# Batch 0 of an FFT-then-GLU kernel: the input in three slices, one sum in column tiles, weight merges placed earlier

## The chip, the cores and the metric

One core of a Trainium2 chip runs the whole program. The metric is device time in microseconds (us). The kernel before took 1947.11 us, the median of three runs (1946.08 to 1948.29). One execution was also taken by the hardware profiler; every duration below is from that execution. The engines are PE (TensorE, matrix products; PEld is its weight loading), DVE (VectorE), ACT (ScalarE), POOL (GpSimd) and SP (SyncE, which here only issues DMAs).

## The reference

For `x` of 8 batches x 3008 positions x 256 features it takes the real part of a two-dimensional Fourier transform (over positions and over features), and sends every resulting row through a gated layer with 1536 hidden features:

```python
X = np.fft.fft(x, axis=1)
X = np.fft.fft(X, axis=2)
x = X.real.astype(np.float32).reshape(B * S, D)
gate = 1.0 / (1.0 + np.exp(-(x @ w_gate)))
out = (gate * (x @ w_val)) @ w_out
```

The three weight matrices come as 8-byte floats.

## The kernel before

**Mathematics.** The transform over features is a 256 x 256 product, so it is multiplied into `w_gate` and `w_val` once: `merge` (L329) makes the tables `G1` and `G2`. The transform over positions is done for each batch: the rows of x are folded (s, S-s, M+s and M-s added and subtracted, M = 1504), and the folded rows are multiplied with a cosine and a sine table `st`, which gives `pk` and `qk`. One feature column (number 128) of the cosine part has no partner; its transform, the row E, is kept apart. For a chunk of 252 frequencies and a tile of 128 hidden features, gate and value are then the sum of three terms: G1 times pk, plus E times a column `ge`, plus or minus G2 times qk. The two signs are the frequency and its mirror image.

**The loop.** The main loop (L917) goes over *steps* i. A step is one tile of 128 of the 1536 hidden features (12 a chunk) for one chunk of one batch. Steps 0 to 11 are the first chunk of batch 0. In a step, PE runs `front_a(i)` (G1 times pk, into a PSUM bank `pf`), `back` (five of the products with `w_out`, into the banks `po`; from step 5 on) and `front_b(i)` (G2 times qk). ACT takes twice the bank between the two (`part`, L616), and after front_b the sigmoid of one sign (`gate_a`, L635); DVE makes the other sign out of both (`z`, L640), multiplies gate and value (`h`, L652), ACT makes the second sigmoid (L653), DVE multiplies again (L654, called *second h* below). When the second h of step i is done, the bank of step i is free. POOL adds blocks of h (`sf`, L660) for a scheme that saves products: seven sums after steps 1, 4, 7..., six after steps 2, 5, 8....

**PSUM.** There are eight banks: three in the pool tagged `x`, used by `pf`, by merges and by the sums of the transform, and five named `po0` to `po4`, which `back` takes from step 5 on. Before that, other work may be put into them (the argument `other`).

**Weights.** There are 18 loads of 512 KB, each a tile of 256 columns of `w_gate` or `w_val`, or 256 rows of `w_out`, in the order of the list `jobs`. A load is made into 4-byte floats by `weight_parts` (two ACT instructions, L297 and L298) and `weight_join` (three DVE instructions, L307, L308 and L310, then one on POOL, L312). `weight_use` then merges it (four products, a copy of each half to SBUF on ACT, L336 and L337, and two small DMAs `ge` that turn row 0 of G2 into columns), or, for `w_out`, queues `forms`, sums of it for the saving scheme.

**Batch 0 in the kernel before.** x comes in two DMAs, the table in two halves each for cosine and sine (`load_table`, L192). DVE and POOL fold it in two halves (`half1`, `half2`). Six sums of the transform follow: for each of two blocks pk, E and qk. E is computed as if its one column were 128 equal ones, so its row stands on all partitions. In steps 0 to 4 E is added by two further products of G2 with a tile that has only row 0 filled; in steps 5 to 11 DVE adds it (`part`, L619, two instructions); from step 12 on ACT writes E times ge into the bank ahead of front_a (`seed`, L600).

**What sets the order.** All engines run their instructions in the order in which the program issues them; nothing reorders them at run time. The order of `pre`, `use` and `side` (L863 to L871) says in which step a join, a merge or a load stands. Loads are issued on SP, also in order; a DMA also waits until the one that used the same one of eight completion counters has landed, so a `ge` that is slow to land holds a load that has its counter.

Of the kernel before, what the change touches and what calls it, by code (L numbers as in the profile page):

```python
# [82 lines left out]
def kernel(  # L83
# [61 lines left out]
    def load_x(b):  # L145
        X[b] = xp.tile([P, 4, NQ, D], F32, name="x4", tag="x4")
        for h in range(0, 4, 2):
            if b:
                nc.sync.dma_start(out=X[b][:, h : h + 2], in_=XR[b][:, h : h + 2])
            else:  # L150
                nc.sync.dma_start(out=X[b][0:NP, h : h + 2], in_=xf[b, :, h : h + 2])
# [29 lines left out]
    G1 = const.tile([P, 2, F], F32, name="G1")  # L181
    G2 = const.tile([P, 2, F], F32, name="G2")
# [9 lines left out]
    def load_table(t, nq):  # L192
        for q in range(0, NQ, nq):
            yield nc.sync.dma_start(out=ST[0][0:NP, t, q : q + nq], in_=stab[:, t, q : q + nq])
# [14 lines left out]
    def table_odd():  # L209
# [21 lines left out]
        def tangent():  # L231
# [8 lines left out]
    jobs = [(0, 0), (1, 0), (0, 1), (1, 1), (2, 0), (0, 2), (1, 2), (2, 1), (0, 3), (1, 3), (0, 4), (2, 2),  # L240
            (1, 4), (0, 5), (1, 5), (2, 3), (2, 4), (2, 5)]
    RAW, WS = {}, {}
    shared = {}
    KEEP = 10

    def weight_load(j):


        w, c = jobs[j]
        src = (moe_w_gate, moe_w_val, moe_w_out)[w]  # L250
        src = src[2 * c * P : 2 * (c + 1) * P, :] if w == 2 else src[:, c * WC : (c + 1) * WC]
        src = src.rearrange("(c p) f -> p c f", p=P)

        def some(n, pool, tag):

            if tag not in shared:
                shared[tag] = pool.tile([P, n * WC], F32, name=f"w{tag}", tag=tag)
            return shared[tag]

        def home(j):  # L260

            if j in (0, 1, 2, 3, 5):
                if j > 2:
                    ws = some(5, pqp, "qk")[:, (j // 5) * 2 * WC : (j // 5 + 1) * 2 * WC]
                    return sp.tile([P, 4 * WC], F32, name="raw", tag="sf"), ws
                t = hp.tile([P, 6 * WC], F32, name="raw", tag="h")
                return t[:, 0 : 4 * WC], t[:, 4 * WC :]
            if j in (4, 6, 9):
                t = wf[:, {4: 1, 6: 2, 9: 3}[j]].rearrange("p m n -> p (m n)")
                return t[:, 0 : 4 * WC], t[:, 4 * WC : 6 * WC]  # L270
            t = some(10, cp, "c")
            if j == 7:
                raw = pqp.tile([P, 4 * WC], F32, name="raw", tag="pk")
                return raw, t[:, 6 * WC : 8 * WC]
            return t[:, 0 : 4 * WC], t[:, 4 * WC : 6 * WC]

        if j < KEEP:
            raw, ws = home(j)
        else:
            both = some(24, xp, "x4").rearrange("p (i n) -> p i n", n=2 * WC)  # L280
            r, i = (j - KEEP) % 3 * 2, 6 + (j - KEEP) % 6
            raw, ws = both[:, r : r + 2].rearrange("p a n -> p (a n)"), both[:, i]
        raw = raw.bitcast(I32).rearrange("p (c f w) -> p c f w", c=2, w=2)
        ws = ws.rearrange("p (c f) -> p c f", c=2)
        WS[j] = ws
        if src.dtype == F32:
            nc.sync.dma_start(out=ws, in_=src)
        else:
            RAW[j] = raw
            nc.sync.dma_start(out=raw.rearrange("p c f w -> p c (f w)"), in_=src.bitcast(I32))  # L290
# [38 lines left out]
    def merge(ws, g, c, other):  # L329
# [6 lines left out]
        nc.scalar.copy(G2[:, g, cs], ps[:, WC : 2 * WC])  # L336
        nc.scalar.copy(G1[:, g, cs], ps[:, 0:WC])  # L337
# [48 lines left out]
    def fold_ops(b, nq):  # L386
# [51 lines left out]
        else:  # L438

            def half1(q):  # L440
                point(nc.vector, 2, 3, q)
                first(nc.vector, 2, 3, q)
                for blk in range(2):
                    across(nc.vector, blk, q)
                    feat(nc.vector, *parts[blk], q)

            def half2(q):
                across(nc.vector, 0, q)
                feat(nc.vector, *parts[0], q)
                across(pool, 1, q)  # L450
                feat(pool, *parts[1], q)
            for q in qs:
                point(nc.vector, 0, 1, q)
            first(nc.vector, 0, 1, slice(0, NQ))
            point(pool, 2, 3, qs[1])
            first(pool, 2, 3, qs[1])
            ops += [lambda: half1(qs[0]), lambda: half2(qs[1])]
        for blk, (v, r) in enumerate(parts):
            if b and blk:
                W[b, blk] = v[:, :, HD:D], r[:, :, HD:D]  # L460
                continue
            W[b, blk] = (v[:, :, 0:HD], r[:, :, 0:HD],
                         v[:, :, HD : HD + 1].to_broadcast([v.shape[0], NQ, P]))
# [56 lines left out]
    def seq_start(b):  # L520
        PQE[b] = [pqp.tile([P, NK + 1], F32, name=name, tag=name) for name in ("pk", "qk")]
        if not b:
            PQE[b].append(op.tile([P, NK + 1], F32, name="ek", tag="os"))
# [5 lines left out]


# [60 lines left out]
    N1 = 5  # L591

    def seed(i):
# [5 lines left out]
        for g in range(2 if i >= NFT else 0):  # L599
            nc.scalar.activation(PF[i][:, g], EK[i // NFT], AF.Copy, scale=ge[:, g, f : f + 1])  # L600

    def front_a(i):
        (pk, *_), ks, _, _, fs = cut(i)
        if i < NFT:
            seed(i)
        for g in range(2):
            mm(PF[i][:, g], G1[:, g, fs], pk[:, ks], i < NFT and g == 0, True)
        for g in range(2 if i < N1 else 0):
            mm(PF[i][:, g], G2[:, g, fs], shared["qk"][:, 4 * WC : 4 * WC + CH], False, True)

    def part(i):
# [3 lines left out]
        if not N1 <= i < NFT:  # L615
            nc.scalar.activation(AP[i], PF[i], AF.Copy, scale=2.0)  # L616
            return
        for g in range(2):
            nc.vector.scalar_tensor_tensor(out=AP[i][:, g], in0=pqe[2][:, ks],  # L619
                                           scalar=ge[:, g, f : f + 1], in1=PF[i][:, g],  # L620
                                           op0=ALU.mult, op1=ALU.add)
# [6 lines left out]
    def gate_a(i):  # L628
# [7 lines left out]
        if N1 <= i < NFT:  # L636
            nc.vector.scalar_tensor_tensor(out=z[:, :, ::-1], in0=AP.pop(i), scalar=2.0, in1=PF[i],
                                           op0=ALU.mult, op1=ALU.subtract)
        else:
            nc.vector.tensor_tensor(z[:, :, ::-1], AP.pop(i), PF[i], op=ALU.subtract)  # L640
# [6 lines left out]
    def gate_b(i):  # L647
# [5 lines left out]
        nc.scalar.activation(pf[:, 0], z[:, 0], AF.Sigmoid)  # L653
        nc.vector.tensor_tensor(h[:, fh, n:], pf[:, 0], z[:, 1], op=ALU.mult)  # L654
# [145 lines left out]

    nc.gpsimd.memset(nil, 0.0)
# [3 lines left out]
    for j in range(2):  # L805
        weight_load(j)
    load_x(0)
    for _ in load_table(0, NQ // 2):
        pass
    for j in range(2, 5):  # L810
        weight_load(j)
    sines = load_table(1, NQ // 2)
    next(sines)
    for j in range(5, 7):
        weight_load(j)
    next(sines)
    for j in range(7, KEEP):
        weight_load(j)

    def weight_round(*js):  # L820
        for j in js:
            weight_parts(j)
            weight_join(j)

    weight_parts(0)
    weight_parts(1)
    weight_join(0)
    weight_join(1)
    weight_use(0)
    weight_use(1)  # L830
    seq_start(0)

    e0 = shared["qk"][:, 4 * WC : 4 * WC + CH]
    nc.gpsimd.memset(e0, 0.0)
    other = {(0, 0): (4, None), (0, 1): (4, None), (0, 2): (0, 1), (1, 2): (2, 3)}
    cos = [seq_group(0, blk, what, other.get((blk, what))) for blk in range(2) for what in (0, 2)]
    for i, f in enumerate(fold_ops(0, NQ // 2)):
        f()
        for sums, _, _ in cos:
            sums(*range(i * NQ // 2, (i + 1) * NQ // 2))  # L840
    sin = [seq_group(0, blk, 1, other.get((blk, 1))) for blk in range(2)]
    for i in range(2):
        for sums, _, _ in sin:
            sums(*range(i * NQ // 2, (i + 1) * NQ // 2))
    evacuate = [then for _, then, _ in cos + sin]
    for then, js in zip(evacuate, ((2, 3), (4,), (5,), (6,), (7,), (8,))):
        weight_round(*js)
        then()()
    nc.scalar.dma_start(out=ed[0:1], in_=PQE[0][2][0:1])
    nc.vector.tensor_copy(e0[0:1], PQE[0][2][0:1, 0:CH])  # L850
    weight_parts(9)
    for j in range(KEEP, KEEP + 3):
        weight_load(j)
    weight_use(2)
# [8 lines left out]
    pre, use = {}, {}  # L863
    for j, i in enumerate((0, 1, 2, 3, 4, 5, 6, 7, 9), 9):
        if i:
            pre.setdefault(i - 1, []).append(lambda j=j: weight_parts(j))
        pre.setdefault(i, []).insert(0, lambda j=j: weight_join(j))
        if KEEP <= j < len(jobs) - 3:
            at(i, lambda j=j: weight_load(j + 3))
    for j, i in enumerate((0, 0, 1, 2, 0, 3, 4, 5, 4, 6, 7, 8, 8, 8, 11), 3):  # L870
        use.setdefault(i, []).append(lambda j=j: weight_use(j))  # L871
    at(N1 - 1, lambda: nc.vector.tensor_copy(PQE[0][1][0:1, 0:CH], PQE[0][2][0:1, 0:CH]))
# [17 lines left out]
    for i in range(i0, count, i0):  # L890
        at(i - 8, lambda i=i: e_rows(i))
# [25 lines left out]
    for i in range(count):  # L917
        front_a(i)
        if N1 <= i < NFT:
            part(i)  # L920
        if i:
            gate_a(i - 1)
        if not N1 <= i < NFT:
            part(i)
        if i0 <= i + 1 < count:
            seed(i + 1)
        if i:
            gate_b(i - 1)
# [67 lines left out]
```

## Time and profile before

| | |
|---|---|
| Median of three runs | 1947.11 us |
| The profiled execution's own time | 1951.1 us |
| Its span | 1949.0 us |
| PE busy | 1917.7 us (98% of the span) |
| POOL, DVE, ACT busy | 82%, 75%, 68% |
| PE busy in the first 1/40 of the span (48.7 us) | 6 tenths |
| Start of the first front_a, step 0 | 52.57 us |
| Start of front_b of step 14 | 120.88 us |
| One step where PE never waits | 3.125 us |

The page divides the span into 40 slices. PE is busy for nine tenths or more in all but the first. From 121 us on, the chain that ended last is PE alone for a long way: eight matmul records of `pf` (1.70 us) and ten of `po` (1.43 us) in turn, 3.125 us a step. A product of 4-byte floats is recorded as two matmuls, so "x8" is four products.

### The profile page before, as it was taken

How to read it: one execution, taken by the hardware profiler on the slowest of the kernel's cores; microseconds unless marked ns; L12 is line 12 of the kernel's file. 1: busy time of each engine (PE TensorE's matmuls, PEld its weight loads, DVE VectorE, ACT ScalarE, POOL GpSimd, SP SyncE). 2: the span in 40 equal slices, each digit the busy share in tenths (PEclk: the TensorE clock that was granted, in tenths of full speed). 3: DMA queues.
4: the chain of work that ended last, by engine and by line, in shares of the span. 5: the costliest groups of instructions: out<-in, count | busy, mean ns of one | idle time of the engine just before them, and what ended most of it. 6: DMA issues, size and time to landing. Idle time of an engine off the chain costs nothing.

```text
span 1949.0 us, 34556 instructions
## 1 busy us (share of the span) xinstructions
PE 1917.7 (98%) x11262; PEld 1789.8 (92%) x11262; DVE 1461.0 (75%) x3269; ACT 1332.5 (68%) x3125; POOL 1589.7 (82%) x2842
## 2 busy tenths in 40 slices
PE   6999999999999999999999999999999999999999
PEld 3789889999999999999999999999999999999998
DVE  6777787787777777777777777777777777776776
ACT  3567757776777677776777767777677776777775
POOL 3779998997889878987889878888788886777775
PEclk8999999999999999999999999999999999999999
DMA  8352513212012120222012021221210110011101
GB/s 270 90 145 20 118 32 111 47 25 82 14 47 58 17 79 14 57 49 79 14 25 78 18 79 23 45 53 20 82 20 14 19 23 14 14 20 22 25 16 31
DMA packets 168565, 97.85 MB, mean 50 GB/s; under 512 B 131803, under 2 KB 160070, under 8 KB 165838
## 3 DMA queue, kind: packets, MB, share of 16 engines
q1 hardware_dynamic: 167254, 95.12, 20.5%
q8 instruction: 91, 1.49, 0.3%
q14 instruction: 88, 0.72, 0.1%
q10 hardware_dynamic: 1100, 0.51, 0.1%
q0 software_dynamic: 32, 0.00, 0.0%
HBM read 70.35 MB, written 47.24 MB: 60 GB/s over the span
## 4 chain that ended last, share of the span: by engine, by line
PE 92%; DVE 4%; DMA 2%; ACT 1%; issue 0%; SPq 0%; ACTq 0%; DVEq 0%
PE pf L135 48%; PE po L135 40%; PE ev L135 3%; DMA st<-in_stab_dram 1%; DVE c L754 1%; PE od L135 1%; DMA ge<-G 1%; PE ps L135 1%; DVE z L640 1%; ACT pf L653 0%; DVE h L654 0%; DVE h L652 0%; PE row L135 0%; DVE wf L375 0%; DMA raw<-in_moe_w_val_dram 0%
## 5 line engine op out<-in xcount | busy, mean ns | idle before, releaser
L660 POOL TENSOR_TENSOR sf<-h 128x168 f32<-128x168 f32 (+1 forms) x955 | 530.8, 574 | 225.1 <-DVE h L654 225.0
L660 POOL TENSOR_TENSOR sf<-h,sf 128x168 f32<-128x168 f32 (+1 forms) x1146 | 638.4, 576 | 61.5 <-DVE h L654 60.9
L135 PE MATMUL pf<-qk,G 128*128 128x252 f32 (+1 forms) x2304 | 583.2, 376 | 4.2 <-DVE ae L619 2.3
L135 PE MATMUL pf<-pk,G 128*128 128x252 f32 (+1 forms) x2304 | 583.5, 376 | 1.6 <-DVE h L654 1.4
L654 DVE TENSOR_TENSOR h<-pf,z 128x252 f32<-128x252 f32 (+1 forms) x576 | 241.5, 419 | 420.0 <-ACT pf L653 420.0
L600 ACT ACTIVATE pf<-ek,ge 128x252 f32<-128x252 f32 (+1 forms) x1128 | 531.4, 471 | 18.7 <-DVE h L654 0.2
L135 PE MATMUL po<-sf,wf 128*128 128x168 f32 (+1 forms) x3056 | 527.5, 305 | 0.0
L616 ACT ACTIVATE ae<-pf 128x504 f32<-128x504 f32 (+1 forms) x569 | 335.0, 589 | 233.8 <-PE pf L135 232.5
L135 PEld LDWEIGHTS pf<-pk,G 128*128 128x128 f32 x2304 | 436.1, 190 | 55.7 <-DVE h L654 3.2
L135 PEld LDWEIGHTS po<-sf,wf 128*128 128x128 f32 x3056 | 470.4, 190 | 8.2
L135 PE MATMUL po<-h,wf 128*128 128x168 f32 (+1 forms) x2674 | 473.9, 306 | 0.2 <-DVE wf L372 0.2
L754 DVE TENSOR_TENSOR c<-c 128x168 f32<-128x168 f32 (+1 forms) x949 | 450.6, 506 | 5.2
L135 PEld LDWEIGHTS po<-h,wf 128*128 128x128 f32 x2674 | 425.5, 190 | 17.2 <-DVE wf L372 0.6
L135 PEld LDWEIGHTS pf<-qk,G 128*128 128x128 f32 x2304 | 409.9, 190 | 31.6 <-ACT ae L616 3.1
L640 DVE TENSOR_TENSOR z<-ae,pf 128x504 f32<-128x504 f32 (+1 forms) x569 | 378.4, 665 | 25.0 <-ACT h L635 23.4
L635 ACT ACTIVATE h<-pf 128x252 f32<-128x252 f32 (+1 forms) x576 | 217.7, 378 | 155.5 <-PE pf L135 147.8
L653 ACT ACTIVATE pf<-z 128x252 f32<-128x252 f32 (+1 forms) x576 | 214.4, 372 | 113.7 <-DVE h L652 111.1
L652 DVE TENSOR_TENSOR h<-h,pf 128x252 f32<-128x252 f32 (+1 forms) x576 | 232.3, 403 | 0.0
L660 POOL TENSOR_TENSOR sf<-sf 128x168 f32<-128x168 f32 (+1 forms) x191 | 109.5, 573 | 15.0
L660 POOL TENSOR_TENSOR sf<-sf,h 128x168 f32<-128x168 f32 (+1 forms) x191 | 104.2, 545 | 0.0
L135 PE MATMUL ev<-st,x 63*128 63x189 f32 (+3 forms) x372 | 73.1, 347 | 9.4 <-DVE x L403 6.6
L688 ACT COPY c<-po 128x504 f32<-128x504 f32 (+1 forms) x144 | 81.7, 568 | 0.0
(148 smaller groups left out, 888.8 us busy)
## 6 DMA issues: line engine op xcount, KB each, us to landing
x<-xr SPq DMA_DIRECT2D x14, 1536.0 KB
out_dram<-os SPq DMA_DIRECT2D x376, 56.0 KB
xr<-in_xf_dram SPq DMA_DIRECT2D x14, 768.0 KB
xr<-in_xf_dram SPq DMA_DIRECT2D x35, 256.0 KB
ek<-ed SPq DMA_DIRECT2D x39, 126.0 KB
out_dram<-os SPq DMA_DIRECT2D x288, 7.0 KB
st<-in_stab_dram SPq DMA_DIRECT2D x4, 1111.9 KB
x<-in_xf_dram SPq DMA_DIRECT2D x2, 1512.0 KB
```

Of the source, the lines that this page charges most:

```text
L135: nc.tensor.matmul(o, l, r, start=start, stop=stop, skip_group_check=True)
L600: nc.scalar.activation(PF[i][:, g], EK[i // NFT], AF.Copy, scale=ge[:, g, f : f + 1])
L616: nc.scalar.activation(AP[i], PF[i], AF.Copy, scale=2.0)
L635: nc.scalar.activation(H[p][:, fh, 0:n], PF[i][:, 0], AF.Sigmoid)
L640: nc.vector.tensor_tensor(z[:, :, ::-1], AP.pop(i), PF[i], op=ALU.subtract)
L652: nc.vector.tensor_tensor(h[:, fh, 0:n], h[:, fh, 0:n], pf[:, 1], op=ALU.mult)
L653: nc.scalar.activation(pf[:, 0], z[:, 0], AF.Sigmoid)
L654: nc.vector.tensor_tensor(h[:, fh, n:], pf[:, 0], z[:, 1], op=ALU.mult)
L660: nc.gpsimd.tensor_tensor(block(p, dst), block(p, a), block(p, b), op=(ALU.subtract, ALU.add)[op])
L688: (nc.vector.tensor_copy if t == 1 or t == 3 and not last else nc.scalar.copy)(C[0][:, 3 * t * R : 3 * (t + 1) * R], PO[t][:, 0 : 3 * R])
L754: engine.tensor_tensor(t[:, dst * R : (dst + 1) * R], *v, op=(ALU.subtract, ALU.add)[op])
```

## The change

It touches only batch 0, up to step 11; from there on the two programs issue the same work in the same order, but for the prefetch of the E rows.

- **x and table.** x comes in three DMAs by pairs of slots (`load_third`, all 128 rows), each followed by its part of the cosine table in two DMAs (112 and 14 rows). A fold of a third is all on DVE (`third`, `feats`), and the products of that third follow it at once.
- **E.** Its sums take one column as stationary operand and go to four column tiles of one bank (`e0_sums`). The four rows are copied (`e0_copies`), put together (`e0_row`) and spread over all partitions by a product with a row of ones (`e0_spread`). The products with G2 in steps 0 to 4 and the DVE additions in steps 5 to 11 are gone; every step is seeded by ACT, one step ahead.
- **PE before the data.** Twelve products on a tile of ones stand ahead of the first merge and two behind the second (`warm`).
- **Sines.** The sums for qk stand in three parts between the first three front_a.
- **Order of loads and merges.** The two first w_out tiles move behind (0, 2) and (1, 2) in `jobs`, twelve loads have homes of their own instead of ten, and loads 6 to 11 are issued ahead of the `ge` of merge 4. A merge copies both halves of its bank in one instruction. Merges 0 to 5 stand ahead of step 0, 8 to 14 in steps 1 to 7; the first three of them in `po2` and `po3`, the others in the pool `x`.
- **Joins in the loop** stand between the first and the second h of the step before (`gate_b(i, between)`).

```diff
-        for h in range(0, 4, 2):
-            if b:
...
+    def load_third(j):
+        q = slice(2 * j, 2 * j + 2)
+        rows = xf.rearrange("b p h q d -> (b p) h q d")
+        nc.sync.dma_start(out=X[0][:, :, q], in_=rows[0:P, :, q])
...
-    KEEP = 10
+    KEEP = 12
...
-        nc.scalar.copy(G2[:, g, cs], ps[:, WC : 2 * WC])
-        nc.scalar.copy(G1[:, g, cs], ps[:, 0:WC])
+        nc.scalar.copy(G[:, :, g, cs], ps.rearrange("p (h n) -> p h n", h=2))
...
+            def third(q):
+                a, m = x4[:, 0:3:2, q], x4[:, 1:4:2, q]
+                tt(a[:, :, :, 1:D], a[:, :, :, 1:D], m[:, :, :, D - 1 : 0 : -1], op=ALU.add)
+                tt(a[:, :, :, 0], a[:, :, :, 0], m[:, :, :, 0], op=ALU.add)
+                across(nc.vector, 0, q)
+                across(nc.vector, 1, q)
+            def feats(q):
+                v, r = x4[:, 0:2, q], x4[:, 2:4, q]
+                nc.vector.memset(r[:, :, :, 0:1], 0.0)
+                lo, hi = v[:, :, :, 1:HD], v[:, :, :, D - 1 : HD : -1]
+                tt(r[:, :, :, 1:HD], lo, hi, op=ALU.subtract)
+                tt(lo, lo, hi, op=ALU.add)
...
+    def e0_sums(j):
+        if not j:
+            E0["ps"] = bank("pe", NB - 1)
+        for q in (2 * j, 2 * j + 1):
+            for blk in range(2):
+                c0, n = ((0, NE), (NE, NO))[blk]
+                row = (2 * blk + q % 2) * TB
+                mm(E0["ps"][row : row + 1, 0:n], W[0, blk][2][:, q], ST[0][0:NP, 0, q, c0 : c0 + n],
+                   not j, j == N3 - 1)
...
+    def e0_spread():
+        ps = bank("ek", NB - 1)[:, 0:CH]
+        mm(ps, busy[0:1, 0:P], shared["er"][:, 0:CH], True, True)
+        EK[0] = ekp.tile([P, CH], F32, name="ek", tag="ek")
+        nc.scalar.copy(EK[0], ps)
...
     def front_a(i):
         (pk, *_), ks, _, _, fs = cut(i)
-        if i < NFT:
-            seed(i)
         for g in range(2):
-            mm(PF[i][:, g], G1[:, g, fs], pk[:, ks], i < NFT and g == 0, True)
-        for g in range(2 if i < N1 else 0):
-            mm(PF[i][:, g], G2[:, g, fs], shared["qk"][:, 4 * WC : 4 * WC + CH], False, True)
+            mm(PF[i][:, g], G1[:, g, fs], pk[:, ks], False, True)
...
-    def gate_b(i):
+    def gate_b(i, between=()):
...
         nc.scalar.activation(pf[:, 0], z[:, 0], AF.Sigmoid)
+        for f in between:
+            f()
         nc.vector.tensor_tensor(h[:, fh, n:], pf[:, 0], z[:, 1], op=ALU.mult)
...
+    warm(12)
     weight_parts(0)
     weight_parts(1)
     weight_join(0)
+    weight_use(0)
     weight_join(1)
-    weight_use(0)
     weight_use(1)
     seq_start(0)
...
+    warm(2)
+    for j in range(N3):
+        folds[2 * j]()
+        e0_sums(j)
+        folds[2 * j + 1]()
+        if j == N3 - 1:
+            e0_copies()
+            e0_row()
+        for sums, _, _ in cos:
+            sums(2 * j, 2 * j + 1)
+        if j < 2:
+            weight_round(2 + j)
+    e0_spread()
+    put = [then() for _, then, _ in cos]
+    for f in put:
         f()
+    weight_load(5)
+    load_table(1, 2)
+    for j in range(6, KEEP):
+        weight_load(j)
...
+    sines(0)
+    first(0)
+    weight_round(4, False)
+    sines(1)
+    weight_use(4, 4)
+    first(1)
+    weight_round(5, False)
+    weight_parts(6)
+    weight_join(6)
+    sines(2)
+    for _, then, _ in sin:
         then()()
+    first(2)
...
+    weight_use(5, 4)
+    weight_use(6)
+    weight_parts(7)
+    weight_join(7)
+    weight_use(7)
+    weight_parts(8)
...
-    pre, use = {}, {}
-    for j, i in enumerate((0, 1, 2, 3, 4, 5, 6, 7, 9), 9):
+    pre, use, mid = {}, {}, {}
+    for j, i in ((8, 0), (9, 1), (12, 2), (10, 3), (11, 4), (13, 5), (14, 6), (15, 7), (16, 8), (17, 9)):
         if i:
             pre.setdefault(i - 1, []).append(lambda j=j: weight_parts(j))
-        pre.setdefault(i, []).insert(0, lambda j=j: weight_join(j))
+        mid.setdefault(i, []).append(lambda j=j: weight_join(j))
...
+    for j, i, other in ((8, 1, 2), (9, 2, 3), (12, 2, None), (10, 4, 2), (11, 5, None), (13, 6, None), (14, 7, None),
+                        (15, 7, None), (16, 8, None), (17, 9, None)):
+        use.setdefault(i, []).append(lambda j=j, other=other: weight_use(j, other))
...
-        front_a(i)
-        if N1 <= i < NFT:
-            part(i)
+        if i >= N3:
+            front_a(i)
         if i:
             gate_a(i - 1)
-        if not N1 <= i < NFT:
+        if i >= N3:
             part(i)
+        elif i == 1:
+            part(2)
-        if i0 <= i + 1 < count:
+        if N3 <= i + 1 < count:
             seed(i + 1)
         if i:
-            gate_b(i - 1)
+            gate_b(i - 1, mid.pop(i, []))
```

## The prediction

> **What bounds the kernel now.** First the page's top and its slices, to see how much the change can reach.
>
> ```profile
> span 1949.0 us, 34556 instructions
> PE 1917.7 (98%) x11262; PEld 1789.8 (92%) x11262; DVE 1461.0 (75%) x3269; ACT 1332.5 (68%) x3125; POOL 1589.7 (82%) x2842
> PE   6999999999999999999999999999999999999999
> PEclk8999999999999999999999999999999999999999
> ```
>
> Only the first slice (48.7 us) has PE open, and from step 14 on PE never waits (a pair of 1.70 and 1.43, 3.125 us a step). So the change is worth what it moves the start of front_b of step 14, 120.88 us now, and nothing else; everything later shifts with it. Next the chain of waits up to there, and the PE timeline, whose brackets hold the idle time ahead and what ended it.
>
> ```profile
> 8.70 6.70 PE L135 MATMUL ps<-raw,dt 128*128 128x256 f32 x16 [8.70 <-POOL raw L312]
> 25.46 1.43 PE L135 MATMUL ev<-st,x 126*128 126x377 f32 x4
> 45.48 1.63 PE L135 MATMUL ev<-st,x 126*128 126x377 f32 x2 [2.78 <-DMA st<-in_stab_dram]
> 77.62 1.96 PE L135 MATMUL ps<-wx,dt 128*128 128x256 f32 x8 [1.88 <-ACT G L337]
> 107.44 1.12 PE L135 MATMUL pf<-qk,G 128*128 128x252 f32 x4 [2.35 <-DVE ae L619]
> ```
>
> Three limits in turn: loads and folds up to 22 us (sums start at 21.96), the sine table at 45.48, and in the steps the chain of ACT, DVE and POOL that makes weights and gates. Last the windows around the two longest waits, and the groups of a weight join in the steps (window 55 to 108 us). The windows give each engine's busy time, the granted clock, the DMA share and GB/s.
>
> ```profile
> 44.00:46.00 2.00, 0.52 (x1) 0.50 (x2) 0.32 (x1) 0.00 (x0) 0.82 (x1) 0.87 0.86 310
> 46.00:48.00 2.00, 2.00 (x4) 1.01 (x3) 0.71 (x2) 1.44 (x3) 0.00 (x0) 0.50 0.24 91
> 48.00:50.00 2.00, 2.00 (x6) 1.15 (x5) 1.40 (x4) 1.29 (x3) 1.00 (x1) 0.78 0.04 13
> 104.00:108.00 4.00, 1.65 (x11) 1.35 (x10) 3.93 (x8) 0.00 (x0) 3.92 (x7) 1.00 0.66 218
> ```
>
> ```profile
> L307 DVE TENSOR_SCALAR wx<-wx 128x512 f32<-128x512 f32 x8 | 4.7, 590 | 0.0
> L308 DVE TENSOR_SCALAR wx<-wx 128x512 int32<-128x512 int32 x8 | 4.7, 582 | 0.3
> L310 DVE SCALAR_TENSOR_TENSOR wx<-wx 128x512 int32<-128x512 int32 x8 | 7.6, 949 | 0.3
> L312 POOL TENSOR_TENSOR wx<-wx 128x512 int32<-128x512 int32 x8 | 10.9, 1369 | 6.1 <-DVE wx L310 6.1
> ```
>
> A join is 2.12 us of DVE here (0.590 + 0.582 + 0.949), but 1.55 where POOL is quiet (0.43, 0.43, 0.69), and then 1.3 of POOL.
>
> **The change, part by part.** I lay the new order of each engine along the queues and give every instruction its duration from a row of before. The same walk over before's steps 0 to 8 ends 1.5 to 3 us ahead of its trace, so it flatters.
>
> *Start.* Twelve products of 0.42 (the first ones at half rate) end about 8.2, where PE was idle to 8.70; were the weights there sooner, they would cost up to those 5 us. Merge 0 at 8.7 then takes 1.70 at full clock; 16 records took 6.70 with merge 1, which now waits for POOL (13.2). This saves PE time that was idle time anyway: the folds come later.
>
> *Loads and folds.* Before moved 274, 327 and 311 GB/s in the first three stretches of 10 us. Counting bytes in the order of issue, third 0 has landed (2.36 MB) at about 10, third 1 (4.69 MB) at 16, third 2 (7.02 MB) at 23. A third costs DVE 1.27 + 0.17 + 1.28 + 0.06 + 1.28 = 4.05 (765 elements took 0.95, 768 as much; scaled). With joins 2 and 3 between, DVE folds at 10.1, 17.3 and 23.3, ends 27.4. The extra DMA issues (0.34 us each on SP, twelve table halves for four) lie ahead of data that the bandwidth holds back; uncovered, three of them would cost 1.
>
> *Sums and E.* E shrinks from 12 products of 0.63 to four small ones a third, 0.71 (24 such records, three thirds' worth, took 2.13 at 203.28; no row shows less, and run one by one at 0.63 they would take 2.5, 1.8 more on the path for the last third; I take the row of the same shape), four copies of 0.43, rows 2.0 and a spread of 0.43, beside the cosine sums (2.51 a third), which end at 29.9. DVE places E and pk until 33.2, so sines begin at once behind step 0's needs: first front_a ends 35.0. Merges 4 and 5 wait 1.7 and 2.3 for joins behind DVE's places. Front_b of step 0 starts at 50.9, against 56.05: -5.15.
>
> *Steps 0 to 4.* Removed: ten products with row 0 of G2 (five steps x 0.85 = 4.25 of PE). Added: seeds, 2 x 0.49 of ACT a step, behind ACT's own waits. But merges now wait: merge 8 for two weight parts on ACT (4 x 0.57), two joins and POOL (idle 5.0, starts 56.7); merge 9 for join 9, which stands between the first and second h (3.1); merge 10 for POOL, where seven sums (7 x 0.67), forms (1.18) and L312 (1.37) follow the second h of step 1 (4.8). Front_b of step 4 ends 75.7; before 74.9. So -5.15 has become +0.8.
>
> *Steps 5 to 7.* The DVE additions (2 x 0.465 a step) go to ACT, and both G copies become one (0.57 for 0.74). What is late next: the seed of step i+1 already holds the third bank of the pool x, so a merge in step i needs the bank of step i-1, which comes free at its second h. From front_b's end: h 0.41, z 0.6, h 0.41, the join put between 2.12, second h 0.42, with handoffs 4.1, of which the next front_a covers 0.85: idle 3.2. With merge 1.70, po 1.43 and front_b 0.85 a step is 8.05. Before, where DVE alone set the pace, front_b ended at 82.0, 88.3, 94.2; now at 83.8, 91.8, 99.9. That is +5.7.
>
> *Steps 8 to 14.* One step of 3.1, one of 4.8, then 3.26 each; before lost time here to L619 (2.35 at 107.44). Front_b of step 14 at 123.0, against 120.88: +2.1. All later work is the same; E rows fetched three steps earlier and the row's write on SP lie where the DMA engines are not full (share 0.66 at 104 to 108); without that room they would cost SP an issue each, 0.34.
>
> *The clock.* The 2.78 us of idle ahead of 45.48 was followed by a granted clock of 0.50 and 0.78; the six products behind it took 5.58 for 6 x 0.628 = 3.77, a fall of 1.8 us. After 1.88 and 2.35 of idle (77.62 and 107.44) the clock stayed 1.00. New idles of 5.0 (merge 8, mostly hidden, as POOL is later anyway), 3.1, 4.8 and three of 3.2 lie above the first. How many fall isn't to be had from before: between none (0) and all (six, +10.8). I take one on the path, +1.8, as other idles stand only just above 2.78 and not every slot is alike.
>
> The Trainium skill, page "TensorE: Matmul & The Clock Gate", section "HAM oscillation — how this bites in real kernels", says that PE should have no idle gap over about 3.4 us, else it goes back to half rate. The trace has a fall after 2.78, below that bound, and agrees with no fall at 2.35. By the page only 5.0 and 4.8 fall, which is my sum; by the trace's row those of 3.1 and 3.2 fall as well, which is the second case below.
>
> Sum: +2.1 + 1.8 = +3.9, so the profiled execution's 1951.1 (span 1949.0) would become 1955.0. It stands 4.0 over the median of 1947.11; carried to the median, 1951.0.
>
> **The rivals.** 0.2% (3.9 us) is about what a measurement can tell from no change.
>
> *The clock falls in steps 5 to 7 too.* Three more of 1.8: +9.3, 1956.4. For it: 2.78 sufficed at 45 us. Against: each of these idles is 3.2 only if a join takes its longer time.
>
> *Late ge's hold the third slice.* Before, ge's issued at 12.9 to 16.9 landed only 9 to 10 us later behind the big loads (the chain holds one of 10.55). A load that needs their completion counter waits; then third 2 lands near 26 and DVE starts on it 2.7 later than at 23.3: +6.6 in all, 1953.7. Against: fewer bytes are queued ahead of them now.
>
> *Faster: merges don't wait.* Place: merges 10, 11, 13, 14, which I give 14.4 us of idle (4.8 and three of 3.2). If DVE gets the second h done ahead of the join, or POOL its sums early, they wait as before's own merges did (0.9 each, 3.6): -10.8, so 3.9 - 10.8 = -6.9, 1940.2. The change is a gain as soon as the four together idle under 14.4 - 3.9 = 10.5. For it: PE loses 4.25 of work and DVE 2 x 0.465 a step, and the front is 5.15 ahead. Against: the order of bank use that I read from the issue order.
>
> *Joins undisturbed by POOL* at 1.55, and no clock fall: the same walk ends at -1.7, 1945.4.
>
> **How the numbers follow.** Forecast 0.40 (its own range 1948.5 to 1955: without the clock fall and with one wait shorter by 0.7, or with two falls more; it lies on the bound of 0.2%, and as the walk flatters I put 0.25 above it and 0.15 within); clock 0.15, slower; late ge's 0.07, slower; faster rival 0.30; quiet joins 0.08, within 0.2%. So faster 0.30, same 0.15 + 0.08 = 0.23, slower 0.25 + 0.15 + 0.07 = 0.47. The range reaches from 1938, where the faster rival's four merges wait 0.3 each (3.9 - 13.2 = -9.3), to 1958, the clock case with half of the late ge's 2.7.
>
> **What the profile after would show.** Step 0's front_b near 50.9 and the six front sums done by 46: the front part right; past 54, wrong. The timeline of PE with brackets of 3 us naming DVE's second h (L654) ahead of the merges of steps 5 to 7: the main step right; brackets under 1 us, or naming POOL, and it fails. Front_b of step 14 at 123 to 125 for the forecast, near 114 for the faster rival. The granted clock of 65 to 100 us below 0.9 in several windows: the clock case. DMA in the chain of waits between 22 and 28: late ge's. I would be wrong above all if DVE's joins finish in the shadow of ACT's sigmoid.

## The result, and the profile after

The changed kernel takes 1963.20 us (median of four runs, 1960.97 to 1965.05) against 1947.11: the ratio is 1.0082, interval 1.0064 to 1.0099. It is slower by 16.1 us. The direction was forecast, the size was not: 1951.0 was predicted, with 1958 as the upper end.

The top of the page of the changed kernel, its busy shares and its slices of 49.1 us:

```profile
span 1963.3 us, 34590 instructions
PE 1922.3 (98%) x11272; PEld 1791.4 (91%) x11272; DVE 1452.5 (74%) x3258; ACT 1347.9 (69%) x3147; POOL 1585.0 (81%) x2835
PE   7699999999999999999999999999999999999999
PEclk9799999999999999999999999999999999999999
```

PE is busier than before in the first slice (7 tenths for 6) and has a second slice of 6, with a granted clock of 7 tenths in it. From there on both kernels run alike: front_b of step 14 starts at 135.19, 14.3 us after the 120.88 of before, and PE's last product starts 14.5 later (1956.76 for 1942.25). The two spans differ by 14.3 (1963.3 and 1949.0), so all of it is lost before 135 us. The timeline of PE of the changed kernel (start, duration, what; in brackets the idle time ahead and what ended it) shows where, with the front_b of steps 0, 4 and 14 beside the merges. In the changed kernel L316 is the last instruction of a join, on POOL, and L677 the second h:

```profile
53.66 3.15 PE L135 MATMUL ps<-raw,dt 128*128 128x256 f32 x8
56.60 1.49 PE L135 MATMUL pf<-qk,G 128*128 128x252 f32 x4
63.60 3.78 PE L135 MATMUL ps<-wf,dt 128*128 128x256 f32 x8 [5.51 <-POOL wf L316]
80.06 3.78 PE L135 MATMUL ps<-wf,dt 128*128 128x256 f32 x8 [5.24 <-POOL wf L316]
83.64 1.62 PE L135 MATMUL pf<-qk,G 128*128 128x252 f32 x4
88.72 3.43 PE L135 MATMUL ps<-wc,dt 128*128 128x256 f32 x8 [2.61 <-DVE h L677]
97.88 3.14 PE L135 MATMUL ps<-wx,dt 128*128 128x256 f32 x8 [2.61 <-DVE h L677]
107.26 1.97 PE L135 MATMUL ps<-wx,dt 128*128 128x256 f32 x8 [2.61 <-DVE h L677]
135.19 1.01 PE L135 MATMUL pf<-qk,G 128*128 128x252 f32 x4
```

Two things are to be seen. The idle times stand where the walk put them, ahead of merges 8, 10, 11, 13 and 14 (5.5, 5.2 and three of 2.6; forecast 5.0, 4.8 and three of 3.2); the 3.1 that it put ahead of merge 9 as well didn't come. And five of the six merges shown take 3.1 to 3.8 us instead of 1.9: they run at half rate for all or most of their time. Windows of 3.41 us of the changed kernel (PE busy in the first column after the length; the granted clock is the third number from the end) and the half-rate stretch behind the first of them:

```profile
50.75:54.16 3.41, 1.45 (x7) 1.31 (x8) 3.34 (x6) 1.88 (x5) 1.78 (x2) 1.00 0.66 187
57.57:60.98 3.41, 0.52 (x3) 0.12 (x1) 2.84 (x5) 2.50 (x6) 1.20 (x1) 1.00 0.04 0
84.87:88.28 3.41, 1.24 (x6) 0.76 (x4) 2.50 (x6) 2.48 (x6) 0.48 (x1) 1.00 0.04 0
105.33:108.74 3.41, 1.48 (x7) 1.35 (x8) 1.72 (x4) 2.26 (x5) 1.30 (x1) 1.00 0.22 86
54.20:57.50 3.30, 3.30 (x10) 2.60 (x9) 1.16 (x3) 0.65 (x2) 0.75 (x1) 0.50 0.77 287
```

Cut into windows of 0.1 us, the clock of this trace changes between 10 and 160 us at 54.2, 57.6, 61.0, 67.8, 78.1, 84.9, 88.3, 91.7, 98.5 and 101.9 only, all whole multiples of 3.41 us apart, to about 0.1. Below, *a fall* is such a change from 1.00 to 0.50. In this trace the clock falls where PE was busy for 1.45 us or less of the 3.41 before, and stays where it was busy for 1.48 (the wait of 2.61 ahead of 107.26, which began in the window before that one). PE is busy for 18.8 us in the five stretches at 0.50, so up to 9.4 us are lost; the forecast had one fall, 1.8.

### The profile page after: what moved, and what is told of

Read it like the earlier page. It is cut to its first block, busy times and chain, and to the rows that moved or that the text cites. A ratio compares the mean times of both kernels' runs of the same rounds, so it can differ in the third digit from the quotient of the medians.

```text
span 1963.3 us, 34590 instructions
## 1 busy us (share of the span) xinstructions
PE 1922.3 (98%) x11272; PEld 1791.4 (91%) x11272; DVE 1452.5 (74%) x3258; ACT 1347.9 (69%) x3147; POOL 1585.0 (81%) x2835
## 4 chain that ended last, share of the span: by engine, by line
PE 93%; DVE 4%; ACT 1%; POOL 1%; issue 1%; DMA 0%; ACTq 0%; SPq 0%; DVEq 0%; POOLq 0%
PE pf L135 48%; PE po L135 40%; PE ev L135 3%; PE ps L135 1%; DVE c L777 1%; PE od L135 1%; DVE z L661 1%; DVE h L677 0%; DVE h L673 0%; ACT pf L674 0%; PE row L135 0%; DMA raw<-in_moe_w_val_dram 0%; POOL raw L316 0%; DVE wf L375 0%; ACT pf L635 0%
## 5 line engine op out<-in xcount | busy, mean ns | idle before, releaser
L635 ACT ACTIVATE pf<-ek,ge 128x252 f32<-128x252 f32 (+1 forms) x1152 | 543.0, 471 | 19.5 <-DVE h L677 0.7
L677 DVE TENSOR_TENSOR h<-pf,z 128x252 f32<-128x252 f32 (+1 forms) x576 | 241.5, 419 | 418.7 <-ACT pf L674 418.7
L646 ACT ACTIVATE ae<-pf 128x504 f32<-128x504 f32 (+1 forms) x576 | 339.6, 590 | 235.2 <-PE pf L135 233.0
L661 DVE TENSOR_TENSOR z<-ae,pf 128x504 f32<-128x504 f32 (+1 forms) x576 | 383.3, 666 | 43.0 <-ACT h L660 41.5
L674 ACT ACTIVATE pf<-z 128x252 f32<-128x252 f32 (+1 forms) x576 | 214.3, 372 | 94.2 <-DVE h L673 91.6
L786 DVE STREAM_TRANSPOSE os<-c 128x256 f32<-128x256 f32 x188 | 72.1, 421 | 0.7 <-issue 0.6
```

Of the source, the lines that this page charges most:

```text
L786: nc.vector.transpose(os_[0][:, s, 0:nb, h, :], t[:, c0 : c0 + nb * TB])
```

## The experiments

Each run's time is told as its distance from the kernel before on the same chip, whose median there was 1945.2 to 1946.2; the changed kernel's is +16.1. "Step 14" is the start of its front_b in the profiled execution (changed kernel 135.19).

### Filling PE's idle time

```diff
+        if n and PO:
+            fill(n, PO[0], False)
+        elif n:
+            fill(n, bank("fill", 0), True)
...
+    FILLS = {8: 16, 10: 15, 11: 7, 13: 7, 14: 7}
...
+    fill(5, bank("fill", 4), True)
     first(2)
```

> The changed kernel, with products of a tile of zeros (168 columns, 0.29 us each) put into PE's queue where it stood idle: 16 ahead of merge 8, 15 ahead of merge 10, 7 ahead of each of merges 11, 13 and 14, 5 ahead of the front_a of step 2. They add nothing to any result. Clock theory: in the changed kernel's trace the granted clock is 0.50 in five stretches between 54.2 and 101.9 us, in which PE is busy for 18.8 us, so 9.4 us are lost; with the idle time filled the stretches go, and the time falls by 7 to 9.4, to 1954 to 1956. Rival, that the waits for joins and gates set the pace and the slow products only lie beside them: 1961 to 1965, with the waits ahead of the merges longer by what the products save.

Measured: 1958.28, +13.0. Step 14 starts at 128.29, 6.9 sooner, and its four runs lie within 1.0 us of each other (those of the changed kernel within 4.1). The same stretches of this run's trace:

```profile
61.00:67.70 6.70, 4.17 (x19) 3.24 (x18) 5.19 (x11) 5.53 (x13) 5.24 (x6) 1.00 0.03 3
78.10:84.80 6.70, 5.29 (x30) 4.67 (x28) 5.88 (x11) 3.88 (x8) 5.02 (x8) 1.00 0.02 0
98.60:101.90 3.30, 2.69 (x15) 2.31 (x15) 1.53 (x4) 2.07 (x5) 1.30 (x1) 1.00 0.30 114
```

The clock is 1.00 in all of them, though more work is done. So the falls are a cost of their own, 6.9 us in the profiled executions and 3.1 between the distances of the medians. The median moved less than the 7 to 9.4 expected. From step 0 to step 14 this run takes 72.7 us (55.61 to 128.29) and has no fall there (its only one is at 22.1, in the front): the walk, which has none either, gave 72.1.

### The waits ahead of merges 11, 13 and 14

```diff
-            gate_b(i - 1, mid.pop(i, []))
+            gate_b(i - 1)
```

> The changed kernel with the joins of the loop behind the second h instead of between the first and the second (one call in another place). Theory: merges 11, 13 and 14 wait 2.61 us each for the second h, which waits for the join's 2.1 on DVE; without it they wait about 0.5, and the two falls of the clock there (3.2 us lost) go too: 6.3 + 3.2 = 9.5 less, near 1954. Rival: the join is late instead, the same merges wait for POOL's part of it, and the time stays at 1961 to 1965.

Measured: 1970.06, +24.8. The theory fails: the join behind the second h takes only 0.2 off the wait, the wait ahead of merge 10 grows from 5.2 to 7.1, and a wait of 3.6 comes at 118.94. ACT and PE of this run, around the same merge:

```profile
87.14 0.97 ACT L635 ACTIVATE pf<-ek,ge 128x252 f32<-128x252 f32 x2
88.05 0.36 ACT L674 ACTIVATE pf<-z 128x252 f32<-128x252 f32 x1
```

```profile
89.01 1.97 PE L135 MATMUL ps<-wc,dt 128*128 128x256 f32 x8 [2.40 <-DVE h L677]
```

The second sigmoid (L674), which the second h needs, stands behind both seeds (L635) on ACT. The join on DVE and the seeds on ACT are two waits side by side, and to take one away shows the other.

```diff
+        late = [lambda: seed(i + 1)] if N3 <= i + 1 < count else []
+        if i >= i0:
+            for f in late:
+                f()
         if i:
-            gate_b(i - 1, mid.pop(i, []))
+            gate_b(i - 1, late if i < i0 else [])
```

> The changed kernel, steps 0 to 11 alone, with the seed of step i+1 behind the second sigmoid of step i-1 on ACT instead of ahead of it, and the joins behind the second h as in the run before. With the joins moved alone the idle time ahead of merges 11, 13 and 14 went from 2.61 only to 2.40, and its second h waited for ACT's second sigmoid, which stood behind the two seeds (0.98). Theory: two waits lay side by side there, the join on DVE and the seeds on ACT; with both away the idle time is 1.4 to 1.7, three times 1 us less, and too short for a fall of the clock: 4 to 6.5 less than the changed kernel, 1957 to 1959. Rival: the idle time stays at 2.4, as z and first h alone take it.

Measured: 1966.63, +21.4. The waits are 1.56, 1.68 and 1.68 and no fall follows them, as expected; but 2.9 us of idle time came at 117.39 (PE waits for ACT's part, L646) with a fall behind it, and in this trace step 0 starts at 58.47, behind a fall at 20.7 in the front. The wait is explained; the time isn't better.

```diff
+        rest = [weight_use(j, None, True) for j in ahead.pop(i, [])]
+        late = rest + ([lambda: seed(i + 1)] if N3 <= i + 1 < count else [])
+        if not rest:
+            for f in late:
+                f()
+            late = []
         if i:
-            gate_b(i - 1, mid.pop(i, []))
+            gate_b(i - 1, late + mid.pop(i, []))
```

> The changed kernel with merges 11, 13 and 14 taking their bank ahead of the seed of the next step: their products stand behind front_a as before, but their copy and then the seed stand behind the second sigmoid on ACT. So the merge gets the bank that is free already, and the seed the one that the second h frees. Theory (the prediction's): these three wait for the bank alone. Then nothing is idle ahead of them, 7.8 us, and the two falls of the clock in steps 5 to 7 (3.2) go: up to 11 less than the changed kernel, 1952 to 1956. Rival: the weights are joined only then, or ACT and DVE need a step's 7.7 us anyway, so that as much idle time stands ahead of front_b or front_a: 1960 to 1964.

Measured: 1954.54, +9.3, with step 14 at 125.35. The timeline of PE in steps 5 to 7 has no bracket left:

```profile
87.23 1.89 PE L135 MATMUL ps<-wc,dt 128*128 128x256 f32 x8
...
92.09 1.89 PE L135 MATMUL ps<-wx,dt 128*128 128x256 f32 x8
...
97.01 1.99 PE L135 MATMUL ps<-wx,dt 128*128 128x256 f32 x8
```

A step takes about 5.0 us here (front_b at 85.21, 90.39, 95.24, 100.26) for 9.8, 9.4 and 7.7. So the bank that the seed had taken was the cause of the wait, as the prediction said. From step 0 to step 14 the run takes 66.6 us for the changed kernel's 78.6, but step 0 is later (58.79 for 56.60), behind two falls in the front. The second of them is the one fall seen that a count of busy time doesn't give:

```profile
34.66:38.07 3.41, 2.44 (x8) 0.91 (x7) 2.00 (x5) 1.97 (x5) 0.00 (x0) 1.00 1.03 250
```

PE is busy for 2.44 us of this window, and the clock is 0.50 from 38.1 to 41.4. Why isn't known.

```diff
+            if j in FILLS:
+                fill(FILLS[j], bank("fill", 0))
+            return merge(WS.pop(j), w, c, other, defer)
...
+    FILLS = {8: 16, 10: 15}
...
+    fill(5, bank("fill", 4))
     first(2)
```

> The changed kernel with two of the single edits together: merges 11, 13 and 14 ahead of the seed, and products of zeros ahead of the front_a of step 2 (5), merge 8 (16) and merge 10 (15). Theory: the clock and the bank are two separate costs, so what is left of the clock's falls after the first edit (two, 9 us of PE at half rate, 4.5 lost) goes with the second: about 4 less than 1954.5, near 1950, and the runs lie within 1.5 of each other. Rival: they are one cost, as the bank's wait made the falls: 1953 to 1955.

Measured: 1950.87, +5.0 (eight runs, 1949.89 to 1952.05, a spread of 2.2 where 1.5 was expected); step 14 at 120.13. The clock is 1.00 throughout:

```profile
10.00:54.00 44.00, 35.26 (x142) 21.09 (x141) 27.91 (x51) 16.23 (x32) 7.48 (x6) 1.00 0.97 282
54.00:110.00 56.00, 48.33 (x260) 42.61 (x258) 45.83 (x81) 40.35 (x92) 41.98 (x57) 1.00 0.18 54
```

Bank and clock are two costs: alone the edits gave 6.8 (with the falls that went with the bank's wait) and 3.1, together 11.1 of the 16.1.

### The front

```diff
-        nc.gpsimd.tensor_tensor(wi, wi, lo, op=ALU.add)
+        (nc.vector if j in (1, 2, 3) else nc.gpsimd).tensor_tensor(wi, wi, lo, op=ALU.add)
```

> The changed kernel with the last instruction of joins 1, 2 and 3 on DVE instead of POOL. Theory: DVE's four-element addition L447 took 1.25 instead of the forecast 0.17 in each third because POOL's addition (2.15 us beside it, 1.28 alone) was running, and ended with it. Then L447 takes 0.2 in all three thirds, at the price of about 0.7 on DVE for each join, merges 1 to 3 start 1 to 1.5 sooner, and front_b of step 0 starts 1 to 3 us before 56.60; the time falls by as much, or by less where the waits in steps 1 to 7 take it back. Rival, that the strided four elements take 1.2 on their own: L447 stays, and front_b of step 0 starts no sooner.

Measured: 1962.18, +16.9. First the changed kernel's DVE and POOL in the second third, then this run's DVE:

```profile
18.40 1.22 DVE L446 TENSOR_TENSOR x<-x 126x1020 f32<-126x1020 f32 x1
19.54 1.24 DVE L447 TENSOR_TENSOR x<-x 126x4 f32<-126x4 f32 x1
```

```profile
18.62 2.13 POOL L316 TENSOR_TENSOR raw<-raw 128x512 int32<-128x512 int32 x1 [6.33 <-DVE raw L314]
```

```profile
18.29 1.22 DVE L446 TENSOR_TENSOR x<-x 126x1020 f32<-126x1020 f32 x1 [0.16 <-DMA x<-in_xf_dram]
19.42 0.16 DVE L447 TENSOR_TENSOR x<-x 126x4 f32<-126x4 f32 x1
```

Four elements took 1.24 us and ended when POOL's addition did (20.78 and 20.75), and POOL took 2.13 instead of the 1.28 that the same addition takes at 42.15. Without POOL it is 0.16, in all three thirds. Front_b of step 0 starts at 55.04 for 56.60, but that isn't the gain of the edit: in the changed kernel the fall at 54.2 slows merge 5, just ahead of it (3.15 us). Two other profiles of the same front as the changed kernel's, without a fall ahead of step 0, start it at 55.22 and 55.25 (the runs with the joins behind the second h and with the parts early). So the edit gained 0.2 here: PE now waits 1.7 us at 21.92 for the cosine table. In the three runs below that have it too and no fall ahead of step 0, that wait is 0.4 to 0.9 and step 0 starts at 53.29 to 53.56, so it can be worth up to 2.0. The time of this run doesn't change.

### Merges 8 and 10

```diff
-    for j, i, other in ((8, 1, 2), (9, 2, 3), (12, 2, None), (10, 4, 2), (11, 5, None), (13, 6, None), (14, 7, None),
+    for j, i, other in ((8, 2, 2), (12, 2, None), (9, 3, 3), (10, 5, None), (11, 6, None), (13, 7, None), (14, 8, None),
```

> The changed kernel with merges 8, 9, 10, 11, 13 and 14 one step later (steps 2, 3, 5, 6, 7, 8 for 1, 2, 4, 5, 6, 7), joins where they are. Theory: merges 8 and 10 wait 5.5 and 5.2 us for POOL's part of their joins only because they stand one step too early; a step later they find it done, and with the two falls of the clock there (4.5 us lost) the time falls by 5 to 12. Merges 11 to 14 wait for a bank, so theirs stay at 2.6. Rival: the order of DVE and ACT, not the place of the merge, sets the pace of steps 0 to 4, so the same idle time stands ahead of front_b or front_a instead: within 2 of 1963.

Measured: 1963.63, +18.3: the rival. PE does front_b of step 1 first and then waits as long (5.1 at 63.09), and merge 10 meets the bank's wait (7.1 at 83.32). The place of the merge isn't what makes it wait.

```diff
     first(2)
+    weight_parts(7)
+    weight_parts(8)
...
-    weight_parts(7)
     weight_join(7)
     weight_use(7)
-    weight_parts(8)
```

> The changed kernel with nothing but the parts of weights 7 and 8 on ACT ahead of the copy of merge 5. Theory: merge 8 waits 5.5 us because these four ACT instructions (2.3 us) stand behind a copy that waits for PE until 56.85; ahead of it they are done by 55.3, and merge 8 starts 3 to 4.5 sooner, too short an idle time for a fall of the clock there: 3 to 6 less than the changed kernel. Rival: DVE, which places qk until 55.3 and then makes two joins, sets merge 8: 1 or less.

Measured: 1963.09, +16.9. The idle time ahead of merge 8 is 4.4 instead of 5.5, so the theory of the ACT queue holds for 1.1 us (1.5 against the 5.94 of the run with the joins behind the second h, where, as here, no product ahead of merge 8 is slowed); a fall still follows.

Five runs looked for a better order. The first moved a w_out tile out of the way of the first gates, on top of the merges ahead of the seed; the second put joins 1 to 3 on DVE besides:

```diff
-    for j, i in ((8, 0), (9, 1), (12, 2), (10, 3), (11, 4), (13, 5), (14, 6), (15, 7), (16, 8), (17, 9)):
+    for j, i in ((8, 0), (7, 1), (9, 2), (12, 3), (10, 4), (11, 5), (13, 6), (14, 7), (15, 8), (16, 9), (17, 10)):
```

> The run before (merges 11, 13 and 14 ahead of the seed) and the parts and the join of the second w_out tile moved from ahead of step 0 into step 1, the other weights of the steps one step later where that is early enough (merge 8 stays in step 1; 9, 10, 11, 13, 14 in 3, 5, 6, 7, 8; the w_out tiles in 2, 4, 8, 9, 10). Theory: merge 8 waits 5.5 us because ACT and DVE do two weights between front_b and the gates of step 0; with one away its wait is 2 to 3 and the gates of steps 0 and 1 come sooner, and merge 10 no longer meets POOL's seven sums: 4 to 9 less than the run before. Rival: the work of ACT, DVE and POOL in steps 0 to 4 is the bound in any order: within 2 of it.

> The run before with the last instruction of joins 1, 2 and 3 on DVE. Theory: the front gains 1.5 us (front_b of step 0 at 55.04 instead of 56.60 when this was done alone), and with the waits of the steps gone it reaches the end: 1 to 2 less than the run before. Rival: the steps take it back: the same.

Measured: 1967.66 and 1966.41, +22.4 and +21.2, 12 to 13 more than the run with the merges ahead of the seed alone. Merge 8's wait fell to 3.1, but merge 10's rose to 6.2 and `back` now waited for its forms (2.87, 2.11 and 2.71 ahead of products with `w_out`, ended by DVE's L380).

The next took three edits together (merges ahead of the seed, parts early, the last instruction of joins on DVE, now of joins 8 and 10 too), and then variations of it (products of zeros; weight 8 ahead of weight 7 and join 11 on DVE):

```diff
+        (nc.vector if j in (1, 2, 3, 8, 10) else nc.gpsimd).tensor_tensor(wi, wi, lo, op=ALU.add)
...
+    weight_parts(7)
+    weight_parts(8)
```

> Three things at once on the changed kernel: merges 11, 13 and 14 ahead of the seed (that run gave 1954.5); the last instruction of joins 1, 2, 3, 8 and 10 on DVE; and the parts of weights 7 and 8 on ACT ahead of the copy of merge 5, which waits for PE. Theory: merge 8's 5.9 us and merge 10's 5.2 us of idle are waits for queues (ACT behind the copy, POOL behind seven sums) and shrink to 1 to 2 each, their falls of the clock go, and the front gains 1.5: 1943 to 1947. Rival: DVE, busy for 9.3 of the 10 us from 70 to 80, has no room for the additions and holds the gates back: 1950 to 1955.

> The run before with products of zeros put ahead of the front_a of step 2 (5), merge 8 (4) and merge 10 (5). Clock theory: if falls are left at these places they go, each worth 1.5 to 2.4; where none is left the filling costs up to 1: 1941 to 1947, and the runs lie closer together. Rival: the same as the run before within 1.

> The three-part run (1950.3) with two of its last long waits taken on: weight 8's parts and join ahead of those of the second w_out tile, whose forms on POOL slowed weight 8's join on DVE (L312 1.39, L314 1.10, L316 1.00 beside them) ahead of 4.6 us of idle before merge 8; and the last instruction of join 11 on DVE, as merge 11 waited 4.4 us for POOL behind its sums. Theory: merge 8 starts right behind front_b of step 0, or 1 to 2 us after, merge 11 2 us sooner, and the two falls of the clock (PE busy for 2 x 2.5 to 3.3 us at half rate) go: 4 to 8 less, 1942 to 1946. Rival: the gates, on ACT and DVE, set the pace of steps 0 to 4, and the same time is idle ahead of merges 9 and 10: 1948 to 1951.

Measured: 1950.30, 1950.57 and 1950.33, so +4.1, +4.4 and +4.8 (ratios 1.0020, 1.0024 and 1.0026, with intervals that together span 1.0011 to 1.0036). None beats the kernel before, and none reaches the 1947 or less that was expected of it. Where a wait was shortened, another grew: in the first, merge 10 waits 1.7 for 5.2, and merge 11 waits 4.4 for POOL; in the last, merge 8 no longer waits, and merge 9 waits 5.9 for POOL.

### The kernel before, once more

> The kernel before, unchanged, for a second profile, as the first one's execution lay 4.0 over the median of its runs. If the clock's falls explain that, this profile has fewer half-rate stretches than the two of the first (18.2 to 25.0 and 45.5 to 48.9) and front_b of step 14 starts up to 3.4 sooner than 120.88; if not, the same stretches, and the difference lies in waits of the first 121 us or behind them.

Measured: 1945.63, -0.2. Its profile has a span of 1944.5 instead of 1949.0, and front_b of step 14 starts at 116.80 instead of 120.88. PE around the place where the first profile had its wait for the sine table:

```profile
44.89 1.43 PE L135 MATMUL od<-st,x 126*128 126x376 f32 x4
46.35 1.97 PE L135 MATMUL ps<-raw,dt 128*128 128x256 f32 x8
...
52.63 1.01 PE L135 MATMUL pf<-qk,G 128*128 128x252 f32 x4
```

The wait of 2.78 and the half-rate stretch behind it aren't there; step 0 starts 3.6 sooner (its front_b at 52.63 for 56.27). There are two half-rate stretches as in the first, and not fewer: one at 18.1 to 24.8 as there, and one at 103.4 to 106.7. The windows ahead of one wait of 2.35, the same in both executions of the kernel before (L619, at 107.44 and 102.52), show why one is followed by a fall and the other is not, first the first profile, then the second with its fall:

```profile
103.41:106.82 3.41, 1.68 (x12) 1.40 (x10) 3.34 (x6) 0.00 (x0) 3.39 (x5) 1.00 0.74 239
```

```profile
99.94:103.35 3.41, 1.06 (x6) 0.77 (x5) 3.34 (x7) 0.00 (x0) 3.33 (x5) 1.00 0.61 196
103.40:106.70 3.30, 3.30 (x12) 2.87 (x11) 2.51 (x6) 1.67 (x4) 1.68 (x3) 0.50 0.48 160
```

The wait is equally long, but in the first it lies across the border of two windows, at 106.82.

## Why the prediction was wrong

The miss is 16.1 - 3.9 = 12.2 us. It comes from three steps.

*The reference.* The prediction made its sum against the one profiled execution and carried it to the median as a constant 4.0. But most of those 4.0 were a wait for the sine table and its fall of the clock, in the very stretch that the change rewrites. (Its 56.05 for step 0 is where the weight load of front_b starts; the first product starts at 56.27.) The -5.15 credited at step 0 was for the larger part a gain on that accident: against the second profile, step 0 of the forecast (50.9) is 1.7 ahead of 52.63, and step 14 (123.0 + 1.8) is 8.0 behind 116.80, not 3.9. That is up to 4.1 of the miss: the medians that go with the two profiles lie 1.5 apart (1947.11 and 1945.63), and how much of the 4.1 goes with that isn't known.

*The clock.* "I take one on the path, +1.8" is the term that was mis-sized. The run with both edits has no half-rate stretch from 10 us on and starts step 0 at 54.64; with the 72.7 of the filled run, step 14 would start at 127.3 without falls. It started at 135.19: 7.9 for the falls, 6.1 more than forecast. The second case (1956.4, chance 0.15) was the right one, and still too small: merges 5, 8 and 10 fell too, and a fall lasts until the border behind a busy window. On the Trainium skill, page "TensorE: Matmul & The Clock Gate", section "HAM oscillation — how this bites in real kernels": its limit of about 3.4 us for a gap isn't what these traces show. Gaps of 2.03, 2.61 and 2.35 were followed by a fall, and one of 2.61 was not; its window of about that length is in the traces, as the grid of 3.41.

*The front.* Step 0 was forecast for 50.9; without any fall it is 54.64 (55.22 and 55.25 in the two profiles named above), 3.7 or more later. A third of the fold was given 4.05 us of DVE and took 5.3, as the walk laid POOL's addition beside DVE's fold without a price. Not all of that lies on the path. The chain that ended last goes, from 8.5 to 31 us, through joins and merges: on it stand POOL's additions of joins 1 and 2 (2.15 and 2.13 for 1.28) and the four-element addition of the last third (1.24 for the walk's 0.17), together 2.8. The trace of before had two rows for the addition of a first column. The walk took the one of 0.16; this is the other, and what POOL did beside it:

```profile
17.97 1.76 DVE L397 TENSOR_TENSOR x<-x 126x3 f32<-126x3 f32 x1
17.14 2.57 POOL L393 TENSOR_TENSOR x<-x 126x765 f32<-126x765 f32 x1 [5.37 <-DMA raw<-in_moe_w_gate_dram]
```

Both end at 19.7. Ahead of step 0 the walk also lacked two waits for seeds on ACT (1.56 and 2.03, ahead of the front_a of steps 1 and 2); it had 2.3 for merge 5 there, which didn't wait. Next behind all this is the cosine table, which the prediction did not time apart from x (PE waits for its second part until 21.92 in the run with the joins on DVE).

The three and the 0.6 by which the steps of the filled run differ from the walk make 14.5. The changed kernel's profiled execution lies 1.9 over its median, which leaves 12.6 for the 12.2. Each term comes from a single execution, so the sum closes to about a microsecond and no better.

What was right: the walk of the steps in its total (72.1 for 72.7; in part by luck, as merge 9's 3.1 didn't come and merge 8 starts 7.0 behind step 0 for 5.8), the places of five of its six waits, and the cause of those of merges 11, 13 and 14, a bank (without its wait, and the falls that went with it, step 14 is 9.8 us sooner). Its inner working was half right: the join does hold the second h, but the two seeds on ACT hold it nearly as long (0.2 less). The faster rival had the right places and failed by their waits: 5.2 + 3 x 2.6 = 13.1, where it needed less than 10.5. That late `ge`s hold the third slice wasn't tested by itself; its sign, DMA in the chain of waits between 22 and 28, isn't in the changed kernel's trace. Why the time stays 5 us over the kernel before with bank and clock both mended wasn't settled by an edit. Against the second profile of before, that run starts step 0 2.0 later (54.64 for 52.63) and takes 1.3 more to step 14 (65.5 for 64.2); PE's idle time ahead of merges 8 and 10 is still there, filled with products of zeros.

## What to carry to other kernels

Before a sum is made against one profile, ask whether that execution is a usual one: one that lies 4 us over the median may hold an accident, and the first place to look for it is the stretch that the change rewrites. Where the profile has two rows for one instruction, a short one and a long one, see what ran beside each before taking one. An order that leaves PE short waits of 2 to 3 us in a row can cost more than the waits: count PE's busy time over fixed windows, not the length of a gap. And when a wait has two causes side by side, taking one away shows nothing; look at what ended it on the engine behind.

## What the runs showed of the hardware

- The granted clock changed only on a grid of 3.41 us (to within 0.2) in every one of the sixteen traces, from 10 us on (the changed kernel: ten changes from 54.2 to 101.9; the kernel before: 18.2, 25.0, 45.5, 48.9; none in the run with bank and clock mended). Up to 150 us they hold 52 falls to 0.50. In 51 of them PE was busy for 0.0 to 1.5 us of the window before; every window with less than 1.48 brought one, and none with more than 1.52 did, but for the one with 2.44 shown above, which stays open. At 0.50 the clock came back at the first border behind a window with 2.96 us or more, and not behind one with 2.82 or less.
- The grid lies differently against the program in each execution, so the same wait of 2.35 us was followed by a fall in one and not in the other. That this makes the spread of a kernel's times isn't shown: the changed kernel's four runs spread by 4.1 us and those of the filled run by 1.0, but four runs of another kernel with the waits (weight parts early) spread by 1.5, and the eight of the run without a fall in its profile by 2.2.
- DVE's addition of 4 elements a partition took 1.24 us beside a POOL addition of 512 integers a partition and ended with it, 0.16 without; POOL's took 2.13 beside DVE's fold for 1.28 alone. In the kernel before, one of 3 elements took 1.76 beside a POOL addition of 2.57 and ended with it.
